# A fused attention and feed-forward kernel: full-array sums, two products in separate banks, differences on GpSimd, a fourth up pair and a split last block

## The chip, the cores and the metric

The kernel runs on one core of one Trainium2 chip. The metric is the device time of one execution in microseconds (us); lower is better. "Span" is the time from the first to the last instruction of the profiled execution, some 1 to 2 us less than the device time of the same run.

## The reference, cut to what matters

Attention with keys and values averaged over groups of 8 tokens, then a feed-forward block whose activation is `h * cos(h)`.

```python
k_p = k.reshape(B, H, Sp, pool, D).mean(axis=3)          # B=8, H=8, S=576, D=64, pool=8: 72 pooled keys
v_p = v.reshape(B, H, Sp, pool, D).mean(axis=3)
attn = softmax(q @ k_p.T / sqrt(D))                      # per batch and head
x = (attn @ v_p).transpose(0, 2, 1, 3).reshape(4608, 512)
h = x @ w_in                                             # 512 -> 2048
out = (h * cos(h)) @ w_out                               # 2048 -> 512
```

## The kernel before

The 4608 tokens go through in nine stages of 512. In a stage the tokens go *up* (64 matmuls of 128x512, 8 groups of 2 banks of PSUM, each group followed by a cosine on ScalarE and a multiply `g_sb` on VectorE) and *down*. From stage 1 on, the down part is a seven-product scheme in place of the eight plain products: sums and differences of quarters of `g_sb` (g1 to g4) times sums and differences of quarters of the weights (w2 to w4). Between the products stands the attention of the next batch, in four units of 4 heads by 256 tokens and a rest of 8 heads by 64: scores, exponential, sums and values, Ln and Exp (which give one over the sum), and the multiply that writes `xT`, the next stage's input. GpSimd loads and pools the keys and values of the batch after.

The buffers of PSUM, and the sums and values. `ones` and `vz` are 64 columns wide here, so two heads sit on the two halves of the output partitions, sums in one bank and values in the other:

```python
    banks = [psum.tile([128, 2, 512], FP32, name=f"bank{i}") for i in range(3)]
    obanks = [psum.tile([128, 512], FP32, name=f"obank{i}") for i in range(2)]
...
    def values_of(parts, later):
        weights = (lambda b, h: ones[:Sp, :]), (lambda b, h: vz[b % 2][:, h // 2, 3 * (h % 2), :])
        for bank in range(2):
            ...
                    nc.tensor.matmul(pair[hp * 64:hp * 64 + 64, bank, ...], lhsT=weights[bank](b, h0 + i), rhs=ex[...])
        ...
            nc.scalar.activation(out=inv, in_=pair[:, 0, 0:w], func=ACTF.Ln)
            nc.scalar.activation(out=inv, in_=inv, func=ACTF.Exp, scale=-1.0)
            later.append(... nc.vector.tensor_mul(out=x_out(b, u, slice(0, 128)), in0=cols(pair[:, 1, :], u), in1=cols(inv, u)))
```

The down part. Four products go to bank A and three to bank B, and the reads between them take partial sums:

```python
        A, Bb = obanks[1], obanks[0]
        products = [(A, True, ...), (A, False, ...), (Bb, True, ...), (A, True, ...), (Bb, False, ...), (A, False, ...), (Bb, False, ...)]
        ...
        reads = [
            lambda: nc.scalar.copy(out=p1, in_=A),
            lambda: nc.scalar.copy(out=o1[:, :, 0:HM], in_=two(A)),
            lambda: add(v16, Bb, p1),
            lambda: add(q15, A, p1),
            lambda: add(o2[:, :, HM:], two(Bb), two(q15)),
            lambda: (add(o1[:, :, HM:], two(A), two(v16)), rows_out(t, 0, o1)),
            lambda: (add(o2[:, :, 0:HM], two(Bb), two(p1)), rows_out(t, 1, o2)),
        ]
```

The softmax here doesn't subtract the row's maximum and nothing guards it: scores larger than these inputs give would overflow.

## Time and profile before

The median was 319.28 us (319.24 to 319.82, 3 runs), the span 318.0 us. The stages, from the first up matmul of one to that of the next:

| part of the span | us |
|---|---|
| start, to the first up matmul | 17.62 |
| stage 0 (no seven products yet) | 35.62 |
| stage 1 (weights combined on VectorE) | 40.00 |
| stages 2 to 6, each | 32.56 |
| stage 7 (little attention left) | 28.06 |
| stage 8, to the end | 33.94 |

A stage is read in two pieces, the up part (13.85 us where nothing holds it) and the rest, called the down part (18.71 us in stages 2 to 6). The page's busy shares and the chain, which the prediction shows, say that TensorE is at work for 91% of the span, and that in a steady stage only three waits of 0.4 to 1.0 us stand in its way. At a change of matmul form the gap is smaller: product 0 starts at 107.08, its 16 matmuls follow at 0.109 us each, up to 108.83, and the scores start at 108.92, 0.09 us later.

### The profile page before, as it was taken

The page shows a single profiled execution, that of the slowest core. Times are in us where ns is not written, and L with a number is a line of the kernel's source. Part 1 is how long each engine was busy: PE and PEld are TensorE (multiplying, and loading weights), DVE is VectorE, ACT ScalarE, POOL GpSimd, SP SyncE. Part 2 cuts the span into 40 slices and gives each one's busy share as a digit, 9 for nine tenths or more (in the row PEclk, how much of TensorE's full clock was granted, in tenths as well). Part 3 has the DMA queues.
Part 4 walks back from the last instruction along what each step waited for, and adds up shares of the span by engine and source line. Part 5 has one row for each costly group of instructions (what it writes and reads, how often), then busy time and mean ns, then how long its engine had stood idle before and what let it go on. Part 6 is the DMA issues. An engine that isn't in the chain of part 4 may idle for free.

```text
span 318.0 us, 5705 instructions
## 1 busy us (share of the span) xinstructions
PE 289.1 (91%) x2320; PEld 180.7 (57%) x2320; DVE 217.7 (68%) x291; ACT 203.7 (64%) x246; POOL 147.4 (46%) x141
## 2 busy tenths in 40 slices
PE   8799999399989997999799989998999899899991
PEld 3445544136764585458645864587457744774580
DVE  5468558999747955695559555995596559647950
ACT  3876993248766777677757776677668766626400
POOL 8362119953992399339943795389600000000000
PEclk9999999869999999999999999999999999999997
DMA  7999995079538872968295919680810050023005
GB/s 157 200 207 207 207 205 127 20 140 141 84 78 150 107 118 66 162 89 136 53 174 70 159 32 188 93 139 14 187 31 0 2 134 2 0 49 85 0 2 132
DMA packets 43850, 32.98 MB, mean 104 GB/s; under 512 B 22064, under 2 KB 38960, under 8 KB 43824
## 3 DMA queue, kind: packets, MB, share of 16 engines
q0 software_dynamic: 19744, 18.07, 36.3%
q1 hardware_dynamic: 24080, 14.56, 22.7%
q8 instruction: 18, 0.29, 0.4%
q14 instruction: 8, 0.07, 0.1%
HBM read 36.70 MB, written 9.44 MB: 145 GB/s over the span
## 4 chain that ended last, share of the span: by engine, by line
PE 73%; DVE 14%; ACT 8%; issue 3%; ACTq 0%; DVEq 0%
PE bank L333 35%; PE obank L409 24%; DVE g_sb L343 5%; PE bank L278 4%; PE obank L346 3%; PE bank L221 2%; ACT cos L340 2%; ACT inv L285 2%; DVE xT L286 2%; ACT inv L284 2%; DVE o_two L417 2%; PE obank L494 1%; DVE w L363 1%; DVE w L362 1%; ACT ex L228 1%
## 5 line engine op out<-in xcount | busy, mean ns | idle before, releaser
L333 PE MATMUL bank<-xT,w_in_sb 128*128 128x512 bf16 x576 | 129.1, 384 | 8.2 <-DVE g_sb L343 4.9
L340 ACT ACTIVATE cos<-bank,half_pi 128x1024 f32<-128x1024 f32 x72 | 79.2, 1113 | 62.9 <-PE bank L333 57.5
L343 DVE TENSOR_TENSOR g_sb<-bank,cos 128x1024 bf16<-128x1024 f32 x72 | 86.6, 1221 | 30.9 <-ACT cos L340 30.9
L333 PEld LDWEIGHTS <-w_in_sb 128*128 128x128 bf16 x576 | 56.5, 98 | 77.4 <-issue 14.2
L150 POOL TENSOR_TENSOR half_sums<-kv_st 72x512 f32<-72x512 bf16 x48 | 59.8, 1271 | 34.1 <-DMA kv_st<-in_k_dram 33.7
L409 PEld LDWEIGHTS <-g 128*128 128x128 bf16 x512 | 49.0, 98 | 7.1 <-issue 1.2
L409 PEld LDWEIGHTS <-g_sb 128*128 128x128 bf16 x384 | 36.7, 97 | 8.8 <-issue 2.3
L228 ACT ACTIVATE ex<-bank 72x1024 bf16<-72x1024 f32 (+1 forms) x40 | 35.6, 928 | 0.8 <-PE bank L221 0.7
L152 POOL TENSOR_TENSOR half_sums<-half_sums 72x512 f32<-72x512 f32 x24 | 33.0, 1396 | 0.0
L284 ACT ACTIVATE inv<-bank 128x512 f32<-128x512 f32 (+1 forms) x31 | 16.7, 538 | 23.9 <-PE bank L278 23.9
L409 PE MATMUL obank<-w_out_sb,g_sb 128*128 128x256 bf16 x256 | 30.7, 272 | 1.0 <-ACT p_sb L419 1.0
L409 PE MATMUL obank<-w,g 128*128 128x256 bf16 x256 | 30.6, 273 | 0.0
L409 PE MATMUL obank<-w_out_sb,g 128*128 128x256 bf16 x256 | 30.6, 273 | 0.0
L286 DVE TENSOR_TENSOR xT<-bank,inv 128x512 bf16<-128x512 f32 (+1 forms) x31 | 19.5, 629 | 11.8 <-ACT inv L285 11.6
L221 PE MATMUL bank<-qT,kk 64*72 64x256 bf16 (+1 forms) x192 | 14.2, 251 | 9.5 <-DVE xT L286 6.2
L314 ACT ACT_TABLE_LOAD x16 | 20.5, 1283 | 1.0 <-PEq L665 0.7
L285 ACT ACTIVATE inv<-inv 128x512 f32<-128x512 f32 (+1 forms) x31 | 18.0, 582 | 1.0
L221 PEld LDWEIGHTS <-kk 64*72 64x72 bf16 x192 | 8.4, 109 | 16.8 <-issue 15.6
L377 DVE TENSOR_TENSOR g<-g,g_sb 128x512 bf16<-128x512 bf16 x32 | 15.5, 484 | 1.1
L155 POOL TENSOR_TENSOR kp<-half_sums 72x512 bf16<-72x512 f32 x12 | 15.7, 1330 | 0.5
L346 PE MATMUL obank<-w_out_sb,g_sb 128*128 128x512 bf16 x64 | 15.7, 380 | 0.0
L417 DVE TENSOR_TENSOR v_sb<-obank,p_sb 128x512 f32<-128x512 f32 x8 | 5.5, 690 | 14.7 <-ACT ex L228 10.7
(80 smaller groups left out, 259.0 us busy)
## 6 DMA issues: line engine op xcount, KB each, us to landing
out_dram<-o_two SPq DMA_DIRECT2D x72, 128.0 KB, 2.4
kv_st<-in_v_dram POOLq DMA_DIRECT2D x8, 576.0 KB, 12.7
kv_st<-in_k_dram POOLq DMA_DIRECT2D x7, 576.0 KB, 7.7
q_b<-in_q_dram POOLq DMA_DIRECT2D x6, 576.0 KB, 9.7
w_in_sb<-in_moe_w_in_dram POOLq DMA_DIRECT2D x4, 512.0 KB, 13.8
w_out_sb<-in_moe_w_out_dram POOLq DMA_DIRECT2D x4, 512.0 KB, 18.2
q_b<-in_q_dram POOLq DMA_DIRECT2D x4, 288.0 KB, 12.5
g_sb<-in_k_dram SPq DMA_DIRECT2D x1, 576.0 KB, 3.5
```

Source lines behind the costliest of these rows:

```text
L150: add(out=s[:, h:h + 2], in0=x[:, h:h + 2, 0:4, :], in1=x[:, h:h + 2, 4:8, :], op=ADD)
L152: add(out=s[:, h:h + 4, 0:2, :], in0=s[:, h:h + 4, 0:2, :], in1=s[:, h:h + 4, 2:4, :], op=ADD)
L221: nc.tensor.matmul(pair[:Sp, bank, c:c + n].rearrange("p (g n) -> p g n", n=64), lhsT=kk[b % 2][half[r], h0 + i, 0:Sp], rhs=att["qT", b][h ...
L228: nc.scalar.activation(out=ex[:, 0:nh * n].rearrange("p (a n) -> p a n", a=2), in_=pair[:Sp, :, 0:nh * n // 2], func=ACTF.Exp, scale=scale ...
L284: nc.scalar.activation(out=inv, in_=pair[:, 0, 0:w], func=ACTF.Ln)
L285: nc.scalar.activation(out=inv, in_=inv, func=ACTF.Exp, scale=-1.0)
L286: later.append(lambda b=b, u=u, pair=pair, inv=inv: nc.vector.tensor_mul(out=x_out(b, u, slice(0, 128)), in0=cols(pair[:, 1, :], u), in1=c ...
L333: nc.tensor.matmul(h[:, j, :], lhsT=w_in_sb[fc // 4][:, ki, (fc % 4) * 128:(fc % 4 + 1) * 128], rhs=xT[:, ki, t * TILE:(t + 1) * TILE], st ...
L340: nc.scalar.activation(out=cos, in_=h, func=ACTF.Sin, bias=half_pi[:, :1])
L343: nc.vector.tensor_mul(out=g_sb[:, 2 * fp:2 * fp + 2, :], in0=h, in1=cos)
L346: nc.tensor.matmul(o, lhsT=g_sb[:, fc, ms * 128:(ms + 1) * 128], rhs=w_out_sb[fc // 4][:, fc % 4, :], start=(fc == 0), stop=(fc == FFCH - 1))
L409: mms.append(lambda bank=bank, first=first, g=g, w=w, fc=fc, p=p: nc.tensor.matmul(bank[:, p * HM:(p + 1) * HM], lhsT=g(fc, p), rhs=w(fc), ...
```

## The change

Its intent: shorten those waits. Sums and values of two heads come from one matmul of 128 columns (`[v | 8]`), two products run in separate banks before any read, the g3 differences leave VectorE, the two output banks serve as a fourth up pair, half the combined weights are made on GpSimd, and the last stage splits its output so that less is left after the last matmul. The core of the diff:

```diff
-    obanks = [psum.tile([128, 512], FP32, name=f"obank{i}") for i in range(2)]
+    opair = psum.tile([128, 2, 512], FP32, name="opair")
+    obanks = [opair[:, i, :] for i in range(2)]
...
     def up_bank(t, fp):
-        return banks[list(up_order(t)).index(fp) % 3]
+        i = list(up_order(t)).index(fp)
+        if t == 0:
+            return banks[i % 3]
+        return (*banks, opair)[i % 4 if i < 7 else 0]
...
-    def put_g3(i):
-        f0, f1 = 4 * i, 4 * i + 4
-        nc.vector.tensor_tensor(out=g3[:, f0:f1], in0=g_part(0, 0, f0, f1), in1=g_part(0, 1, f0, f1), op=SUB)
+    def put_g3(fp):
+        f0, f1 = 2 * fp, 2 * fp + 2
+        nc.gpsimd.tensor_tensor(out=g3[:, f0:f1], in0=g_part(0, 0, f0, f1), in1=g_part(0, 1, f0, f1), op=SUB)
...
-        A, Bb = obanks[1], obanks[0]
+        apart = t == NT - 1
+        if apart:
+            A, Bb = [[banks[i][:, p, 0:HM] for p in range(2)] for i in (1, 2)]
+        else:
+            A, Bb = [[obanks[i][:, p * HM:(p + 1) * HM] for p in range(2)] for i in (1, 0)]
         products = [
             (A, True, part(g_part(0, 0, 0, HF)), of(w_out_sb[0:2])),
-            (A, False, part(g_part(1, 0, 0, HF)), of(w_out_sb[2:4])),
-            (Bb, True, part(g2), of(w2)),
-            (A, True, part(g1), of(w_out_sb[0:2], 1)),
...
+            (Bb, True, part(g_part(1, 0, 0, HF)), of(w_out_sb[2:4])),
+            (A, True, part(g2), of(w2)),
+            (Bb, True, part(g1), of(w_out_sb[0:2], 1)),
...
         reads = [
-            lambda: nc.scalar.copy(out=p1, in_=A),
-            lambda: nc.scalar.copy(out=o1[:, :, 0:HM], in_=two(A)),
...
+            lambda: each(p1, A),
+            lambda: each(o1, Bb, p1, m1, 0),
...
-            if first:
-                values_of(first, later)
-                later.pop(0)()
+            if steady:
+                values(*u2, later)
...
+                if n == 3 and b + 1 < B:
+                    nc.gpsimd.tensor_copy(out=gate, in_=kk[b % 2][0:1, 0, 0:1])
+                    loads(b + 1)
+                if n > 2 and n < 7:
+                    put_g3(n - 3)
```

`values`, which was there before for stage 0, does Ln and the multiply once per half of the partitions. `each` does its copies and adds on VectorE. `gate` is a copy of one element of the pooled keys; it makes GpSimd's queue wait for them before it issues the next loads (in the profile after, 44.7 us of waiting for the transfer of `kk` before its five copies).

More of the change, by code (lines that the diff above doesn't have):

```diff
@@ L267, in values @@
             later.append(mul)
-    def values_of(parts, later):
-        weights = (lambda b, h: ones[:Sp, :]), (lambda b, h: vz[b % 2][:, h // 2, 3 * (h % 2), :])
-        for bank in range(2):
-            for b, u, pair in parts:
-                (c0, n), (h0, nh) = u
-                ex = att["ex", b, u]
-                for i in range(nh):
-                    hp = i % 2
-                    nc.tensor.matmul(pair[hp * 64:hp * 64 + 64, bank, (i // 2) * n:(i // 2 + 1) * n],
-                                     lhsT=weights[bank](b, h0 + i), rhs=ex[:, ex_col(u, i):ex_col(u, i) + n])
-        for b, u, pair in parts:
-            att.pop(("ex", b, u))
-            w = u[1][1] * u[0][1] // 2
-            inv = inverse_tile(w)
-            nc.scalar.activation(out=inv, in_=pair[:, 0, 0:w], func=ACTF.Ln)
-            nc.scalar.activation(out=inv, in_=inv, func=ACTF.Exp, scale=-1.0)
-            later.append(lambda b=b, u=u, pair=pair, inv=inv: nc.vector.tensor_mul(
-                out=x_out(b, u, slice(0, 128)), in0=cols(pair[:, 1, :], u), in1=cols(inv, u)))
     def sums_first(b, u, cs):
@@ L355, in down_out, with put_weights @@
             nc.sync.dma_start(out=rows_of[b_, ORDER[pos]], in_=o[rows])
-    def put_weights():
-        vec = nc.vector.tensor_tensor
-        parts = [[(w[:, :, 0:HM], w[:, :, HM:]) for w in (w_out_sb[i], w_out_sb[i + 2])] for i in range(2)]
-        for i, ((b11, b12), (b21, b22)) in enumerate(parts):
-            yield lambda i=i, x=b22, y=b12: vec(out=w3[i], in0=x, in1=y, op=SUB)
-            yield lambda i=i, y=b11: vec(out=w2[i], in0=w3[i], in1=y, op=ADD)
-            yield lambda i=i, x=b21: vec(out=w4[i], in0=x, in1=w2[i], op=SUB)
+    def put_weights(i, eng):
+        vec = eng.tensor_tensor
+        (b11, b12), (b21, b22) = [(w[:, :, 0:HM], w[:, :, HM:]) for w in (w_out_sb[i], w_out_sb[i + 2])]
+        vec(out=w3[i], in0=b22, in1=b12, op=SUB)
+        vec(out=w2[i], in0=w3[i], in1=b11, op=ADD)
+        vec(out=w4[i], in0=b21, in1=w2[i], op=SUB)
     def put_first_weights(i):
@@ L393, in part @@
             return lambda fc, p: x[:, fc, p * 128:(p + 1) * 128]
-        A, Bb = obanks[1], obanks[0]
+        apart = t == NT - 1
[3 more added lines that the diff above has]
+            A, Bb = [[obanks[i][:, p * HM:(p + 1) * HM] for p in range(2)] for i in (1, 0)]
         products = [
             (A, True, part(g_part(0, 0, 0, HF)), of(w_out_sb[0:2])),
-            (A, False, part(g_part(1, 0, 0, HF)), of(w_out_sb[2:4])),
-            (Bb, True, part(g2), of(w2)),
-            (A, True, part(g1), of(w_out_sb[0:2], 1)),
-            (Bb, False, part(g3), of(w3)),
-            (A, False, part(g4), of(w_out_sb[2:4], 1)),
-            (Bb, False, part(g_part(1, 1, 0, HF)), of(w4)),
+            (Bb, True, part(g_part(1, 0, 0, HF)), of(w_out_sb[2:4])),
+            (A, True, part(g2), of(w2)),
+            (Bb, True, part(g1), of(w_out_sb[0:2], 1)),
+            (A, False, part(g3), of(w3)),
+            (Bb, False, part(g4), of(w_out_sb[2:4], 1)),
+            (A, False, part(g_part(1, 1, 0, HF)), of(w4)),
@@ L404, in down_products @@
         ]
         mms = []
-        for bank, first, g, w in products:
-            for fc in range(HF):
-                for p in range(2):
-                    mms.append(lambda bank=bank, first=first, g=g, w=w, fc=fc, p=p: nc.tensor.matmul(
-                        bank[:, p * HM:(p + 1) * HM], lhsT=g(fc, p), rhs=w(fc),
-                        start=(first and fc == 0 and p == 0), stop=(fc == HF - 1 and p == 1),
-                        skip_group_check=not first))
-        p1, v16, q15 = [msb.tile([128, d_model], FP32, name=n, tag=n, bufs=1) for n in ("p1_sb", "v_sb", "q_sb")]
@@ L415, in down_products @@
-        o1, o2 = [msb.tile([128, 2, d_model], FP32, name="o_two", tag="o_two", bufs=3) for _ in range(2)]
-        two = lambda x: x.rearrange("p (a m) -> p a m", a=2)
-        add = lambda out, in0, in1: nc.vector.tensor_tensor(out=out, in0=in0, in1=in1, op=ADD)
-        reads = [
-            lambda: nc.scalar.copy(out=p1, in_=A),
-            lambda: nc.scalar.copy(out=o1[:, :, 0:HM], in_=two(A)),
-            lambda: add(v16, Bb, p1),
-            lambda: add(q15, A, p1),
-            lambda: add(o2[:, :, HM:], two(Bb), two(q15)),
-            lambda: (add(o1[:, :, HM:], two(A), two(v16)), rows_out(t, 0, o1)),
-            lambda: (add(o2[:, :, 0:HM], two(Bb), two(p1)), rows_out(t, 1, o2)),
+        for n, (bank, first, g, w) in enumerate(products):
+            order = [(fc, p) for fc in range(HF) for p in range(2)]
+            if apart and n == 6:
+                order.sort(key=lambda x: x[1])
+            for fc, p in order:
+                mms.append(lambda bank=bank, first=first, g=g, w=w, fc=fc, p=p: nc.tensor.matmul(
+                    bank[p], lhsT=g(fc, p), rhs=w(fc),
+                    start=(first and fc == 0 and (apart or p == 0)), stop=(fc == HF - 1 and (apart or p == 1)),
+                    skip_group_check=not first))
@@ new lines, in down_products, with each @@
+        p1, v16, q15 = [msb.tile([128, 2, HM], FP32, name=n, tag=n, bufs=1) for n in ("p1_sb", "v_sb", "q_sb")]
+        o1, o2 = [msb.tile([128, 2, d_model], FP32, name="o_two", tag="o_two", bufs=3) for _ in range(2)]
+        m1, m2 = slice(0, HM), slice(HM, d_model)
+        def each(out, bank, other=None, m=slice(0, HM), tk=None):
+            for p in range(2) if apart else (slice(0, 2),):
+                ps = bank[p] if apart else obanks[1 if bank is A else 0].rearrange("p (a m) -> p a m", a=2)
+                if other is None:
+                    nc.vector.tensor_copy(out=out[:, p, m], in_=ps)
+                else:
+                    nc.vector.tensor_tensor(out=out[:, p, m], in0=ps, in1=other[:, p], op=ADD)
+                if apart and tk is not None:
+                    rows_out(t, tk, out, (p,), m, (nc.sync, nc.scalar))
@@ L426, in down_products, with rows_out @@
+        reads = [
+            lambda: each(p1, A),
+            lambda: each(o1, Bb, p1, m1, 0),
+            lambda: each(v16, A, p1),
+            lambda: each(q15, Bb, p1),
+            lambda: each(o2, A, q15, m2, 1),
+            lambda: (each(o1, Bb, v16, m2, 0), apart or rows_out(t, 0, o1)),
+            lambda: (each(o2, A, p1, m1, 1), apart or rows_out(t, 1, o2)),
         ]
         return [mms[i * 2 * HF:(i + 1) * 2 * HF] for i in range(7)], reads
-    def rows_out(t, tk, o):
+    def rows_out(t, tk, o, ps=(0, 1), m=slice(0, d_model), queues=(nc.sync, nc.sync)):
@@ L430, in rows_out @@
         rows_of = out.rearrange("(b p t) m -> b t p m", b=B, t=ROW)
-        for p in range(2):
+        for p in ps:
             for i, rows in enumerate(half):
                 b_, pos = divmod((t * TILE + tk * HT + p * 128) // 64 + i, ROW)
-                nc.sync.dma_start(out=rows_of[b_, ORDER[pos]], in_=o[rows, p])
+                queues[i].dma_start(out=rows_of[b_, ORDER[pos], :, m], in_=o[rows, p, m])
     EX = 4
@@ L525, with loads @@
     sin_tables()
+    def loads(b):
+        load_kv(b, "k", k)
+        load_q(b)
+        load_kv(b, "v", v)
     for t in range(NT):
@@ L547 @@
                 put_first_weights(n // 2 - 1)
-            if 0 < t and n % 2:
-                put_g12(n // 2)
+            if 0 < t:
+                if n % 2:
+                    put_g12(n // 2)
+                if n == 3 and b + 1 < B:
[3 more added lines that the diff above has]
+                    put_g3(n - 3)
             if 0 < t and b < B:
@@ L578 @@
             fi = 0
-            weights = list(put_weights())
             for n, (ms, fc) in enumerate(mms):
@@ L586, with product @@
                     down_out(t, ms, obanks[ms % 2])
-                if n in range(41, 59, 3):
-                    weights.pop(0)()
+                if n == 41:
+                    put_weights(1, nc.vector)
         else:
             products, reads = down_products(t)
-            def product(i):
-                for mm in products[i]:
-                    mm()
+            def product(i, j=0, k=2 * HF):
+                for mm in products[i][j:k]:
+                    mm()
+            if b + 1 < B:
+                pool_add(b + 1, "k")
@@ L596, with scores_of @@
             us = BY_TOKENS
-            steady, rest = b < B, t < B
-            first = [(b, us[i], banks[i]) for i in range(3)] if steady else [(t, REST, banks[1])] if rest else []
-            second = [(b, us[3], banks[0]), (t, REST, banks[1])] if steady else []
-            later = []
-            product(0)
-            reads[0]()
+            later = []
+            u0, u1, u2, u3 = [(b, us[i], banks[j]) for i, j in enumerate((1, 2, 0, 1))]
+            ur = (t, REST, banks[2])
+            def scores_of(*parts):
+                for part in parts:
+                    scores_mm(*part)
+                for part in parts:
+                    scores_exp(*part)
@@ L603, with muls @@
+            def muls():
+                while later:
+                    later.pop(0)()
+            steady, rest = b < B, t < B
             if rest:
                 exp_tables()
-            for part in first:
-                scores_mm(*part)
-            for part in first[:1]:
-                scores_exp(*part)
-            product(1)
+            product(0)
+            product(1, 0, 6)
+            if steady:
+                scores_of(u0, u1, u2)
+            elif rest:
+                scores_of(ur)
@@ L610 @@
+            product(1, 6)
+            reads[0]()
             reads[1]()
-            for part in first[1:]:
-                scores_exp(*part)
-            for i in range(2):
-                put_g3(i)
+            if steady:
+                values(*u0, later)
             product(2)
             reads[2]()
-            put_g4(0)
+            muls()
+            if steady:
+                values(*u1, later)
             product(3)
             reads[3]()
+            muls()
+            put_g4(0)
@@ L620 @@
             put_g4(1)
-            if first:
-                values_of(first, later)
-                later.pop(0)()
+            if steady:
+                values(*u2, later)
             product(4)
             reads[4]()
-            for mul in later:
-                mul()
-            later = []
-            if second:
-                for part in second:
-                    scores_mm(*part)
-                for part in second:
-                    scores_exp(*part)
-            product(5)
@@ L635 @@
-            reads[5]()
-            if second:
-                values_of(second, later)
-                for mul in later:
-                    mul()
+            muls()
+            if steady:
+                scores_of(u3, ur)
+            product(5, 0, 8)
+            if steady:
+                values(*u3, later)
+            elif rest:
+                values(*ur, later)
+            product(5, 8)
+            reads[5]()
+            muls()
+            if steady:
+                values(*ur, later)
@@ L640 @@
+            if b + 1 < B:
+                pool_add(b + 1, "v")
             product(6)
             reads[6]()
+            muls()
         if t < B:
             sin_tables()
-        if 0 < t and b + 1 < B:
-            nc.gpsimd.tensor_copy(out=gate, in_=kk[b % 2][0:1, 0, 0:1])
-        if b + 1 < B:
-            load_kv(b + 1, "k", k)
-            load_q(b + 1)
-            load_kv(b + 1, "v", v)
+        if t == 0:
+            loads(b + 1)
+            put_weights(0, nc.gpsimd)
             pool_add(b + 1, "k")
```

## The prediction

> **What bounds the kernel now.** I read the page first (busy shares, then the chain that ended last), then the chain in order of time, then each engine's timeline over one stage, and last every VectorE instruction with two SBUF inputs against what GpSimd was doing. On the page:
>
> ```profile
> PE 289.1 (91%) x2320; PEld 180.7 (57%) x2320; DVE 217.7 (68%) x291; ACT 203.7 (64%) x246; POOL 147.4 (46%) x141
> PE 73%; DVE 14%; ACT 8%; issue 3%; ACTq 0%; DVEq 0%
> ```
>
> TensorE is the bound on average, but over a quarter of the chain is not TensorE. The chain in time repeats every 32.56 us in the six steady stages (93.23 to 125.80, up to 256.04). One stage:
>
> ```profile
> 93.23 14.02 PE bank L333 x64
> 107.28 1.12 ACT cos L340
> 108.42 1.24 DVE g_sb L343
> 109.70 0.63 PE bank L221 x8
> 110.34 5.40 PE obank L409 x48
> ...
> 119.75 0.61 DVE xT L286
> 120.40 0.33 PE bank L221 x8
> ...
> 124.87 0.42 ACT inv L285
> 125.32 0.44 DVE xT L286
> 125.80 14.02 PE bank L333 x64
> ```
>
> A stage is 13.85 us of up matmuls and 18.72 of down matmuls plus the next batch's attention. TensorE's own work in those 18.72 is some 15.6: seven products of 16 matmuls at 0.109 us (12.25; three follow each other at 110.34, 112.08, 113.83), about 1.0 of scores, 2.1 of sums and values, and small gaps at each change of matmul form. The rest is three waits: 0.38 us for the last `g_sb` multiply before scores (109.70), 1.04 for an `xT` multiply to free a bank (120.40), 0.55 for the last `xT` multiply before the next up (125.80), with their pipeline ends about 3 us a stage. VectorE is busy 21.8 of 32.56 us, ScalarE 23.3.
>
> Two more places. From 51.56 to 61.0 VectorE makes the combined weights, six instructions of 1.27 to 1.75 us, while the up matmuls of stage 1 stand still 4.89 us. And the end: the last matmul is done at 311.18, the last add at 311.89, the span ends at 318.04.
>
> ```profile
> 310.21 4.94 SPq L434 DMA_DIRECT2D out_dram<-o_two  x8
> 311.20 0.69 DVE L417 TENSOR_TENSOR o_two<-obank,p_sb 128x512 f32<-128x512 f32 x1 [1.05 <-PE obank L409]
> ```
>
> The eight last output issues go one after the other from one queue until 315.16, and a landing takes 2.4 us more (page, part 6).
>
> [...]
>
> ```profile
> 63.05 2.48 POOL L152 TENSOR_TENSOR half_sums<-half_sums 72x512 f32<-72x512 f32 x2
> 65.61 1.32 POOL L158 TENSOR_TENSOR vz<-half_sums 72x512 bf16<-72x512 f32 x1
> 64.59 1.23 DVE L376 TENSOR_TENSOR g<-g_sb 128x512 bf16<-128x512 bf16 x1
> 65.85 1.37 DVE L377 TENSOR_TENSOR g<-g,g_sb 128x512 bf16<-128x512 bf16 x1
> ```
>
> Each add, 0.42 us alone, waited for the running GpSimd instruction to end (65.53, 66.93) and finished 0.29 later. Multiplies with one PSUM input kept their 1.22 and 0.69 us beside busy GpSimd. In the stage from 190.92 the adds met GpSimd and VectorE was busy 25.2 instead of 21.8 us, yet the stage still took 32.55: VectorE had slack there. [...]
>
> **The change, part by part.** P is the start of product 0 (107.08 above), 13.85 us after the up start.
>
> *Sums and values over the full array.* 24+24 matmuls with 64 stationary columns, run in pairs, become 24 with 128: 16 at 0.109 and 8 of 64 wide make about 2.0 us against 2.13[...]. The price is on the other engines: sums and values now lie on opposite halves, so Ln and the multiply are done per half. A Ln of 64x512 costs 0.59 as one of 128x512 does, a multiply 0.70 as against 0.69. ScalarE gains 4x0.59+0.37=2.7 us, VectorE 4x0.69+0.43=3.2.
>
> *Two products in separate banks.* Product 1 no longer waits for the copy of product 0. Copy and first add go from ScalarE (0.59+0.57, and a table load of 1.28) to VectorE (2x0.69). Net: ScalarE about +0.3 a stage, nothing.
>
> *Differences on GpSimd.* VectorE loses 2x0.68; GpSimd gains four 128x512 instructions, each an estimate of 1.15 to 1.26 us from its 512-wide adds here. VectorE's net is +3.2+1.4-1.4=+3.2 us, to 25 of 32 us, nearly all in the down part, where it works in order.
>
> *One steady stage by hand, without collisions.* The table is loaded at P+2.6; product 0 and six matmuls of product 1 end at 2.4; scores without a wait (banks 1, 2, 0 free at -0.9, 1.2, 2.6); the three exponentials end at 5.8, Ln and Exp of unit 0 at 7.6. From there VectorE never rests long: four multiplies of 1.31 in spacing, four adds of 0.61, two g4 of 0.64, the last multiply 0.85 make 9.8, and a wait of about 0.2 for unit 3. The next up starts at P+17.65 against 18.72: -1.07. TensorE would have been ready at 15.75.
>
> *The same with GpSimd in the way.* In stages 1 to 5 the differences stand behind the gate and the loads in GpSimd's queue. The gate came 8.9 to 10.6 us after the up start; earlier output issues may make it 8 to 9.7, the three issues take 2.5, so the differences run from 10.4 or 12.2 on, when VectorE does g1 and g2 of the third quarter (13.0), and then the pooling starts (8 us after the gate) and runs to the end of the stage. Third quarter: +0.4 to 1.45. Last quarter: its adds end at about P+5.6 instead of 3.45, the p1 copy at 6.2, product 2 waits for it, and unit 0's multiply starts at 8.8 instead of 7.6. The two g4 take 2.8 instead of 1.3 us (0.57 mean wait, then a whole 1.1, each with 0.55 of own work). Next up at about P+20.0: +1.3 against before.
>
> *Fourth up pair and half the weights on GpSimd.* GpSimd waits 7.78 us for a load before 46.58; three 1024-wide instructions of 2.25 (twice its 512-wide) fit, free. VectorE's weights end at 56.2 instead of 61.0, the multiplies of stage 1 start at 57.4 instead of 62.2, and with four pairs TensorE goes on to its seventh pair unhindered. But the adds then meet the pooling and the differences, so of 4.8 us I keep 1.3 with collisions, 4.6 without.
>
> *Stage 6* has no loads: differences follow their multiplies and slip between the adds, -1.07. *Stage 7*: no wait before scores and none for the p1 copy on ScalarE; 14.2 becomes 13.15, -1.07. *Last blocks apart*: the wait of 0.66 becomes one of 0.8 for the copies in halves, even; but the tail is one 256-wide add (0.42), one issue (0.6) on one of two queues and 2.4 landing, 3.5 against 6.86 us: -3.4.
>
> Sum with collisions: 4x(+1.3) -1.3 -1.07 -1.07 -3.4 = -1.6, 317.6 us. Without: 4x(-1.07) -4.6 -1.07 -1.07 -3.4 = -14.4, 304.9.
>
> **Rivals.** (1) [...] as worked out: 317 to 319. For it: [...] the queue order of the changed kernel puts the differences behind the loads. Against: my gate time is a guess within 2 us; a gate 2 us earlier would let the third quarter through. (2) The collisions mostly miss, or fall into pauses: 305 to 310. For it: before, 3.4 us of them cost nothing. Against: TensorE-side slack is what paid for that, and the change spends it. (3) GpSimd gets late with the pooled keys: its work per stage is 2.5+4.8+9.5+8.2=25 us plus 0.5 per collision, from about 10 us into a stage to 2 us into the next; the keys are due at 6 us into the next, so it should hold; if not, 322 or more. (4) The stage stays TensorE-bound and all waits vanish: 6x3 and the ends, 297; ScalarE's Ln and Exp in a row speak against it.
>
> **Range and chances.** The main account gives 317.6, the other 305. I weigh them about four to one and get 315. The finely split products (6 of 16, 8 of 16) look tuned on a chip, which speaks for a gain that I may underrate. 315.5, range 308 to 321. Under 312.9 is faster by 2%: 0.38; over 325.7: 0.08, through rival 3 alone; within: 0.54.
>
> **What would show it.** Right: in stages 2 to 5 the adds of g1, g2 and g4 take 1 to 1.6 us, VectorE is 25 to 29 us busy, the next up waits for an `xT` multiply at 19 to 20.5 after product 0, stages of 33 to 34.3 us; stage 6 at 31.5; last matmul to end 3.5 us. Wrong: those adds at 0.42 and 0.68, stages under 32, or a wait of `qT` or `kk` before scores.

## The result, and the profile after

The changed kernel is correct and takes 362.64 us (median of 4 runs, 361.29 to 365.23) against 319.26 in the same rounds. The ratio is 1.137 [1.129, 1.144]: it is slower by 14%, and outside the predicted range.

The span grew by 41.4 us to 359.4. Almost every part grew, the ones that the change barely touches included (start and stage 0):

| us | start | stage 0 | 1 | 2 to 5, mean | 6 | 7 | 8 | span |
|---|---|---|---|---|---|---|---|---|
| before | 17.62 | 35.62 | 40.00 | 32.56 | 32.56 | 28.06 | 33.94 | 318.0 |
| after | 19.72 | 42.35 | 42.66 | 38.95 | 35.41 | 32.07 | 31.44 | 359.4 |

Only the last stage is shorter. The page of the changed kernel, busy time of each engine over the span, shows no engine that became a bound by its sum:

```profile
PE 294.6 (82%) x2168; PEld 182.9 (51%) x2168; DVE 247.3 (69%) x326; ACT 205.6 (57%) x254; POOL 189.1 (53%) x176
```

TensorE lost 9 points of its share, and VectorE's share is what it was. So neither is always busy and something makes them wait. The chain that ended last, which carried the reading of before, is no help here: it goes back only to 345.62 us, into the last stage. The waits of TensorE (what waited, on what; us in total, times, longest) give the answer:

```profile
PE opair L398 <- DVE o_two L414: 26.7, 21, 2.7
PE bank L317 <- DVE xT L262: 10.0, 6, 1.7
PE opair L330 <- DVE o_two L335: 5.5, 3, 4.4
PE bank L317 <- DVE g_sb L327: 4.1, 5, 1.5
PE opair L398 <- DVE v_sb L414: 2.8, 7, 0.8
PE opair L398 <- DVE q_sb L414: 2.8, 7, 0.8
```

L398 is the products, L414 the reads of their results. TensorE's products wait 26.7 + 2.8 + 2.8 = 32.3 us for those reads (L330 and L335 are the same pair of roles in stage 0); the kernel before had no such line but 1.0 us on ScalarE's copy. One stage in order of time, first TensorE (start, us, what; in brackets the idle time before and what ended it):

```profile
119.12 2.73 PE L398 MATMUL opair<-w_out_sb,g_sb 128*128 128x256 bf16 x22
...
125.82 1.91 PE L398 MATMUL opair<-w,g 128*128 128x256 bf16 x16 [1.56 <-DVE o_two L414]
127.56 0.60 PE L251 MATMUL bank<-ex,vz 72*128 72x256 bf16 x4
128.51 1.91 PE L398 MATMUL opair<-w_out_sb,g 128*128 128x256 bf16 x16 [0.34 <-DVE v_sb L414]
130.25 0.60 PE L251 MATMUL bank<-ex,vz 72*128 72x256 bf16 x4
131.20 1.91 PE L398 MATMUL opair<-w,g 128*128 128x256 bf16 x16 [0.34 <-DVE q_sb L414]
...
143.61 2.75 PE L317 MATMUL bank<-xT,w_in_sb 128*128 128x512 bf16 x12 [1.67 <-DVE xT L262]
```

and VectorE over the same time:

```profile
121.72 1.43 DVE L359 TENSOR_TENSOR g<-g_sb 128x512 bf16<-128x512 bf16 x1
123.18 1.26 DVE L360 TENSOR_TENSOR g<-g,g_sb 128x512 bf16<-128x512 bf16 x1
124.36 0.68 DVE L412 COPY p_sb<-opair 128x512 f32<-128x512 f32 x1
125.07 0.69 DVE L414 TENSOR_TENSOR o_two<-opair,p_sb 128x512 f32<-128x512 f32 x1
127.76 0.69 DVE L414 TENSOR_TENSOR v_sb<-opair,p_sb 128x512 f32<-128x512 f32 x1 [2.00 <-PE opair L398]
...
130.45 0.69 DVE L414 TENSOR_TENSOR q_sb<-opair,p_sb 128x512 f32<-128x512 f32 x1 [0.57 <-PE opair L398]
```

Follow the clock through both. Product 2 writes the bank that `p_sb` (124.36) read, which was free at 125.04. It starts at 125.82, which is 0.06 us after the end (125.76) of the *other* bank's read, `o_two`. Product 3 writes the bank that `o_two` read, free since 125.76; it starts at 128.51, 0.06 after `v_sb` has read product 2's bank. Product 4 starts 0.06 after `q_sb` has read product 3's. So from product 2 on every product waits for the read of the product just before it. The two banks never work at the same time, and product (1.91) and read (0.69) add up instead of overlapping.

The program that was built says the same. It keeps account of buffers by tile, and two views of one tile share one account. The waits of product 2, for a count of VectorE's instructions, in the programs built from the changed kernel and from e1 below, which has two tiles (these lines are from the built programs, not from the profile; the number is that of the instruction waited for):

```
opair@512  (product 2)   waits for VectorE 285 = o_two <- opair@0,  p1     the other bank's read
obank1@0   (product 2)   waits for VectorE 284 = p1    <- obank1@0         its own bank's read
```

The change does rotate its products through two banks; this trace shows that rotating the addresses is not enough where the waits are kept per tile (product 2 stood 1.56 us, until the other bank's read was done).

The tail, where the kernel before had eight issues in one queue from 310.21 on, now has two queues:

```profile
352.01 4.48 SPq L434 DMA_DIRECT2D out_dram<-o_two  x6
```
```profile
352.02 4.76 ACTq L434 DMA_DIRECT2D out_dram<-o_two  x6
```

The last matmul, by the timeline of TensorE, is done at 354.90, two adds in halves end at 355.69, the issues at 356.78, the span at 359.4: 4.5 us against 6.86 before.

### The profile page after: what moved, and what is told of

Same layout as the page of the kernel before. It is cut to its first block, busy times and chain, and to the rows that moved or that the text cites. A ratio compares the mean times of both kernels' runs of the same rounds, so it can differ in the third digit from the quotient of the medians.

```text
span 359.4 us, 5492 instructions
## 1 busy us (share of the span) xinstructions
PE 294.6 (82%) x2168; PEld 182.9 (51%) x2168; DVE 247.3 (69%) x326; ACT 205.6 (57%) x254; POOL 189.1 (53%) x176
## 3 DMA queue, kind: packets, MB, share of 16 engines
q0 software_dynamic: 19744, 18.07, 32.3%
## 5 line engine op out<-in xcount | busy, mean ns | idle before, releaser
L364 POOL TENSOR_TENSOR g<-g_sb 128x512 bf16<-128x512 bf16 x32 | 38.4, 1208 | 84.1 <-DVE g_sb L327 84.1
L398 PEld LDWEIGHTS <-g 128*128 128x128 bf16 x512 | 51.5, 101 | 40.5 <-issue 32.6
L257 ACT ACTIVATE inv<-bank 64x512 f32<-64x512 f32 (+1 forms) x72 | 39.1, 544 | 41.0 <-PE bank L251 40.1
L262 DVE TENSOR_TENSOR xT<-bank,inv 64x512 bf16<-64x512 f32 (+1 forms) x72 | 45.3, 629 | 6.3 <-ACT inv L258 4.9
L398 PE MATMUL opair<-w_out_sb,g 128*128 128x256 bf16 x224 | 31.6, 295 | 15.9 <-DVE o_two L414 13.1
L398 PEld LDWEIGHTS <-g_sb 128*128 128x128 bf16 x384 | 37.1, 99 | 13.9 <-issue 5.6
L398 PE MATMUL opair<-w,g 128*128 128x256 bf16 x224 | 26.7, 272 | 12.8 <-DVE o_two L414 9.9
L398 PE MATMUL opair<-w_out_sb,g_sb 128*128 128x256 bf16 x224 | 27.6, 273 | 0.6 <-DVE g_sb L327 0.6
L557 POOL COPY gate<-kk 1x1 bf16<-1x1 bf16 x5 | 0.9, 179 | 44.7 <-DMA kk<-kp 44.7
L251 PE MATMUL bank<-ex,vz 72*128 72x256 bf16 (+1 forms) x176 | 21.4, 255 | 0.0
L330 PE MATMUL opair<-w_out_sb,g_sb 128*128 128x512 bf16 x64 | 16.0, 379 | 5.5 <-DVE o_two L335 5.5
L359 DVE TENSOR_TENSOR g<-g_sb 128x512 bf16<-128x512 bf16 x32 | 19.1, 598 | 1.1
L398 PE MATMUL opair<-w,g_sb 128*128 128x256 bf16 x112 | 14.5, 286 | 3.7 <-DVE o_two L414 3.7
```

The source lines that it names most:

```text
L251: nc.tensor.matmul(pair[:, hp, (i // 2) * n:(i // 2 + 1) * n], lhsT=vz[b % 2][:, pj, 2 * hp:2 * hp + 2, :].rearrange("p a d -> p (a d)"), ...
L257: nc.scalar.activation(out=inv[half[1 - hp]], in_=pair[half[1 - hp], hp, 0:w], func=ACTF.Ln)
L262: nc.vector.tensor_mul(out=x_out(b, u, half[hp]), in0=cols(pair[half[hp], hp, :], u), in1=cols(inv[half[1 - hp]], u))
L364: nc.gpsimd.tensor_tensor(out=g3[:, f0:f1], in0=g_part(0, 0, f0, f1), in1=g_part(0, 1, f0, f1), op=SUB)
L398: mms.append(lambda bank=bank, first=first, g=g, w=w, fc=fc, p=p: nc.tensor.matmul(bank[p], lhsT=g(fc, p), rhs=w(fc), start=(first and fc ...
```

## The experiments

Times are medians of 4 runs. The kernel before took 319.39 us (318.63 to 320.83), 319.65, 319.96 and 319.91 in the four sets of rounds. All eleven kernels are correct. The stages of those that the argument uses (spans, one profiled run each):

| us | start | stage 0 | 1 | 2 to 5, mean | 6 | 7 | 8 | span |
|---|---|---|---|---|---|---|---|---|
| e1, two tiles | 17.72 | 35.62 | 42.90 | 36.75 | 34.13 | 28.81 | 31.54 | 337.7 |
| e7, e1 and filler | 17.36 | 36.45 | 42.83 | 35.44 | 32.71 | 27.12 | 31.56 | 329.8 |
| e10, e1, g3 on VectorE | 17.62 | 35.62 | 39.18 | 35.93 | 32.37 | 27.06 | 31.46 | 327.0 |
| e4, e1 and 64-column sums | 16.73 | 36.15 | 42.22 | 33.85 | 32.08 | 27.26 | 31.55 | 321.4 |
| e11, e4, loads after g3 | 17.47 | 35.62 | 37.09 | 34.03 | 33.68 | 27.26 | 31.54 | 318.8 |
| e5, e4, g3 on VectorE | 18.26 | 35.62 | 36.14 | 32.07 | 32.01 | 27.19 | 31.46 | 309.0 |
| e6, e5, multiply first | 17.33 | 36.15 | 35.14 | 31.14 | 30.74 | 27.20 | 31.46 | 302.6 |

My theory after reading the trace was the one tile; the rival was the prediction's own one, collisions of VectorE and GpSimd (an add of 0.42 us alone took 1.23 and 1.37 beside GpSimd's in the kernel before) and the halved Ln and multiply.

### e1: the changed kernel with two tiles again

```diff
-    opair = psum.tile([128, 2, 512], FP32, name="opair")
-    obanks = [opair[:, i, :] for i in range(2)]
+    obanks = [psum.tile([128, 512], FP32, name=f"obank{i}") for i in range(2)]
...
-        return (*banks, opair)[i % 4 if i < 7 else 0]
+        return banks[(i + 2) % 3]
```

> The changed kernel with the two output banks declared as two tiles again, and the up pairs back on three pairs. Theory T1 (one tile makes every product wait for the VectorE read of the OTHER bank): 314 to 322 us, steady stages 33 to 34.3 us as the prediction's collision account had them, no product starting right after the read of the other bank. Rival T2 (the GpSimd/VectorE collisions alone are dearer than I reckoned) and rival T3 (Ln and multiply per half fill ScalarE and VectorE): stays above 350 us, since neither is touched.

Measured: 338.7 us (336.59 to 339.5), ratio to before 1.059 [1.053, 1.064]. The edit takes 23.9 us off, and the start and stage 0 are back at before's lengths (17.72 and 35.62). It changes two things at once, the tile and the fourth up pair; e3 keeps the pair. Of TensorE's waits, those on reads of an output bank are down to the last of these lines, product 2's wait for the copy of its own bank:

```profile
PE bank L316 <- DVE xT L261: 16.5, 6, 2.9
...
PE obank L397 <- DVE p_sb L411: 3.4, 4, 0.8
```

Stage 7, which has almost no attention, shows the cost by itself: its down part takes 32.07 - 13.82 = 18.25 us after and 28.81 - 15.62 = 13.19 in e1, so 5.1 us for five products that wait.

So the one tile is the largest part, but not all: e1 is still 6% slower than before, 17 us above what the theory expected, and the steady stages take 36.75 us and not 33 to 34.3. It waits 16.5 us for the last `xT` multiply before the next up, 2.9 us in a stage.

### e2: the kernel before, with one tile, nothing else changed

```diff
-    obanks = [psum.tile([128, 512], FP32, name=f"obank{i}") for i in range(2)]
+    opair = psum.tile([128, 2, 512], FP32, name="opair")
+    obanks = [opair[:, i, :] for i in range(2)]
```

> The kernel before with only its two output banks put into one tile; nothing else. T1: slower by 2 to 3.5 us in each of six steady stages and by 5 or more in stage 0 and at the end, 340 to 350 us. T2 and T3: 319 us, unchanged.

Measured: 350.67 us (350.37 to 351.24), ratio 1.097 [1.093, 1.101]. The two lines alone cost 31.3 us in the old kernel, 0.7 more than the expected range. By spans the start and stage 0 lose 15.9 of it and stages 2 to 6 lose 2.07 each. Its waits:

```profile
PE opair L347 <- DVE o_two L352: 9.0, 3, 7.8
PE opair L410 <- DVE v_sb L418: 7.4, 8, 1.5
PE opair L410 <- ACT o_two L421: 6.5, 8, 0.9
```

Shown from both sides, then: taking the tile apart helps the new kernel, joining it hurts the old one.

### e3: the fourth up pair without the joint tile

The fourth pair made of two separate tiles, with cosine and multiply of that pair in two halves:

```diff
+        if h is None:
+            for j in range(2):
+                nc.scalar.activation(out=cos[:, j], in_=obanks[j], func=ACTF.Sin, bias=half_pi[:, :1])
+            for j in range(2):
+                nc.vector.tensor_mul(out=g_sb[:, 2 * fp + j, :], in0=obanks[j], in1=cos[:, j])
+            return
```

> The first experiment with the fourth up pair kept, made of the two separate output tiles (cosine and multiply of that pair in two instructions of 512 each). T1: 1 to 3 us faster than with three pairs, mostly in stage 1, where VectorE holds the pairs longest; 313 to 320 us. If the fourth pair itself was the harm, it is slower than the first experiment by over 10 us.

Measured: 335.55 us (334.97 to 336.54), ratio 1.050 [1.046, 1.054]: about 3 us less than e1, as expected of the pair, though with intervals that touch; the time expected, 313 to 320 us, was missed by 15.6. The joint tile was there for this pair: the pair gives 3 us, and with the pair in both kernels the tile takes 27.1 (362.64 to 335.55). The 23.9 of e1 are the difference of the two.

### e4: sums and values with 64 columns again

On e1, each `values` becomes the old form (sums in one bank, values in the other, one Ln and one multiply over 128 partitions), at the new places:

```diff
-                values(*u0, later)
+                values_split(*u0, later)
```

> The first experiment with sums and values as 64-column matmuls again (Ln, Exp and multiply over 128 partitions). T3 in its weaker form (VectorE's order bounds the down part, 3.2 us a stage are from the halves): 1 to 2.5 us a stage faster than the first experiment, 303 to 312 us. If TensorE or the collisions bound it: within 2 us of the first experiment.

Measured: 323.59 us (322.81 to 324.36), ratio 1.013 [1.008, 1.017]. The full-array matmuls with their halved Ln and multiply cost 15.1 us (not tested apart from each other), 2.9 us in each of stages 2 to 5, a little more than the weaker T3 forecast, but from e1's unexpected level, so the time is 11.6 us above the expected range. In e1 VectorE runs without a pause from 157.16 to the next up at 169.79. The end of that row, with multiplies in pairs:

```profile
166.73 1.39 DVE L261 TENSOR_TENSOR xT<-bank,inv 64x512 bf16<-64x512 f32 x2
168.16 0.69 DVE L413 TENSOR_TENSOR o_two<-obank,p_sb 128x512 f32<-128x512 f32 x1
168.88 0.86 DVE L261 TENSOR_TENSOR xT<-bank,inv 64x256 bf16<-64x256 f32 x2
```

The same row in e4, with single multiplies and with pauses in which VectorE waits for TensorE (the next up still waits 1.1 us for the last multiply):

```profile
159.82 0.68 DVE L283 TENSOR_TENSOR xT<-bank,inv 128x512 bf16<-128x512 f32 x1
161.44 0.69 DVE L430 TENSOR_TENSOR o_two<-obank,p_sb 128x512 f32<-128x512 f32 x1 [0.94 <-PE obank L414]
162.04 0.41 DVE L283 TENSOR_TENSOR xT<-bank,inv 128x256 bf16<-128x256 f32 x1
```

This was a cost that the prediction had in its sum; its size is treated below.

### e5: the g3 differences back on VectorE

```diff
-        nc.gpsimd.tensor_tensor(out=g3[:, f0:f1], ...)      # four of 128x512, in the up part
+        nc.vector.tensor_tensor(out=g3[:, f0:f1], ...)      # two of 128x1024, after the second read
```

> The kernel with two tiles and 64-column sums (323.6 us), but with the g3 differences on VectorE in the down part, as before, so that no difference of GpSimd is left; the loads still go out in the middle of the up matmuls. [...] the adds of g1, g2 and g4 take about 0.42 and 0.68 us again wherever GpSimd does not pool, stage 1 comes back to 40 us or under and the steady stages to about 32: 312 to 316 us. Rival: the collisions fall where VectorE has slack, and the two differences put back (2 x 0.68 us a stage) only lengthen its row in the down part: 322 to 330 us.

Measured: 310.32 us (309.86 to 311.02), ratio 0.972 [0.969, 0.974]. It beats the expectation of the first case, that the collisions are what still keeps the kernel behind the one before, by 1.7 us: 13.3 us less than e4, and the first version that beats the kernel before. Stage 1 gains 6.1 us, the steady stages 1.8 each. The mechanism differs a little from the expectation: the differences now meet the pooling themselves and take, in stages 1 to 5, 0.9 to 1.6 us each in place of 0.68. But they do so in the down part, where VectorE has pauses, and the adds of g1 and g2 in the up part are at 0.42 us again with one exception in the steady stages.

### e6: the last multiply before the last add

```diff
-            reads[6]()
             muls()
+            reads[6]()
```

> The kernel of the run before, with one line moved: the last xT multiply goes before the last output add on VectorE. If VectorE's order is what holds the next up matmuls (they waited 1.11 us for that multiply), each of six stages gains about 0.7 to 1.1 us: 4 to 6 us less than the run before, 306 to 311 us. Rival: the multiply itself comes late, from Ln and Exp on ScalarE, and the add in front of it costs nothing: the same time as the run before within 1 us.

Measured: 304.48 us (304.36 to 305.23), ratio 0.954 [0.951, 0.956]. 5.8 us less than e5, 1.5 below the expected range. The waits of the up matmuls for `xT`, 6.7 us in e5, are gone; what is left for them is:

```profile
PE bank L333 <- DVE g_sb L343: 3.9, 6, 1.2
```

This version beats both kernels: 4.6% faster than before, 16% less time than the changed kernel (304.48 against 362.64, medians of different rounds).

### e7: matmuls that nobody reads

In e1's trace the up part, 13.85 us before, took 15.2 to 17.1. The matmuls in it were slow for 3.4 us. By stretches, for the line of the up matmuls (stretch and its length; TensorE's busy time and count; those of its weight loads; granted clock; share of the DMA engines, GB/s):

```profile
132.90:134.20 1.30, 1.28 (x6) 0.60 (x7) 1.00 0.92 203
134.20:137.60 3.40, 3.40 (x9) 1.19 (x8) 0.50 0.98 202
137.60:141.00 3.40, 3.40 (x17) 1.58 (x16) 0.99 0.76 135
```

Nine matmuls in 3.4 us at clock 0.50, and 17 in the same time at 0.99: half of 3.4 us is lost. TensorE had stood still for 2.87 us until 132.92, 1.3 us before this stretch. The test fills the idle time:

```diff
             muls()
+            if steady:
+                for i in range(12):
+                    nc.tensor.matmul(obanks[0], lhsT=w_in_sb[0][:, 0, 0:128], rhs=w_in_sb[0][:, 0, :])
```

> The changed kernel with two tiles (338.7 us), and twelve matmuls of 128x512 after product 6 in each of the six or seven steady stages, into the bank that product 6 does not use; nobody reads them. They only keep TensorE at work while it waits for the last multiply. If the idle of about 3 us before the next up is what halves the granted clock for 3.4 us afterwards, the clock stays at full, each up part takes 13.9 us instead of 15.2 to 17.1, and the kernel takes 328 to 333 us. Rival: the clock falls for another reason[...], so more matmuls do not help: 338 us or more.

Measured: 330.48 us (329.55 to 331.55), ratio 1.034 [1.030, 1.037], 8.2 us less than e1 by doing more work. The up parts took 14.8, 14.8, 15.2, 14.8, 13.9 and 13.9 us in place of 16.1, 16.3, 15.2, 17.1, 15.6 and 15.6; the down parts of stages 2 to 5, 20.55, did not move. What remains above 13.85 is TensorE's wait for late `g_sb` multiplies (6.0 us in all, stage 1 with it). The same place, clock 1.00:

```profile
132.00:135.40 3.40, 3.40 (x16) 1.57 (x17) 1.00 0.90 199
```

The rival, that more matmuls do not help, is out: with more work the mean granted clock of the profiled runs rose from 0.967 to 0.993.

### e8: only the last stage's split, on the kernel before

```diff
-            products, reads = down_products(t)
+            products, reads = (last_products if t == NT - 1 else down_products)(t)
```

`last_products` is the changed kernel's, with the up pairs that are free there.

> The kernel before, with the last stage alone as in the changed kernel: two products in separate banks of the up pairs, output adds in halves, two queues. The prediction took 3.4 us for the tail (6.86 to 3.5 us from the last matmul to the end). If that stands by itself, the last stage goes from 33.94 to about 31 us and the kernel to 315.5 to 317 us, everything before the last stage the same to 0.1 us. Rival: VectorE's halved copies and adds hold up the products by as much as the tail gains: 319 us.

Measured: 317.31 us (316.58 to 318.1), ratio 0.993 [0.990, 0.996]. A gain of 2.3 us, 0.3 short of the expected range. The last stage and the one before it took 59.5 us together in place of 62.0 (one record of an up matmul is missing at their border). In the profiled run the start and stage 1, which the edit does not touch, were also 0.3 and 0.4 us shorter, so "the same to 0.1 us" did not hold. From the last matmul to the end it is 4.5 us, not the 3.5 of the prediction.

### e9: the fourth pair on the best kernel

The edit of e3, on e6.

> The best kernel so far (304.5 us: two tiles, 64-column sums, differences on VectorE, multiply before the last add), with the two output tiles again as a fourth up pair, cosine and multiply in halves there. In the changed kernel with two tiles the fourth pair gave 3.2 us. If it gave that because TensorE could run ahead of a VectorE that collisions had made late, it gives 0 to 1 us here, where the up matmuls run at 13.85 us without a gap: 303.5 to 305. If a fourth pair is worth something by itself, 301 to 303. It costs two smaller instructions in place of one on ScalarE and VectorE, once a stage: at worst 306.

Measured: 304.86 us (304.41 to 305.39), ratio 0.953 [0.950, 0.956]: the same as e6, as the first case expected. In e6, whose up matmuls wait only 3.9 us in all for `g_sb`, the fourth pair is worth nothing.

### e10: halved multiplies without collisions

The edit of e5, on e1.

> The changed kernel with two tiles (338.7 us), keeping Ln and multiply in halves, with the g3 differences on VectorE. With 64-column sums this step took 13.3 us off (323.6 to 310.3). If the two costs add up, 325 to 327 us. If VectorE in its fixed order is the bound with halved multiplies, the two differences of 0.68 us or more put back there eat some of it: 328 to 334 us. If halved multiplies only cost because of collisions, 312 us or under.

Measured: 330.37 us (328.8 to 331.09), ratio 1.033 [1.029, 1.036]. The middle case, 8.3 us. By the spans, stage 1 gives 3.7 us and the up parts, which no longer wait for a late `g_sb` and mostly keep their clock (mean of the span 0.988, in e1 0.967), give 11.2; but the down parts of stages 2 to 5 got longer, from 20.55 to between 20.7 and 22.3 us (4.4 in all), because the two differences now stand in VectorE's full row. So the two costs do not simply add: with halved multiplies VectorE's row is the bound in the down part, and work taken off GpSimd comes back there.

### e11: the differences ahead of the loads

On e4, whose stage 1 held a riddle: an instruction on VectorE (L367, first weights) that takes 0.68 us alone took 3.14. VectorE, then GpSimd, in e4:

```profile
68.24 3.14 DVE L367 TENSOR_TENSOR w_out_sb<-w_out_sb 128x1024 bf16<-128x1024 bf16 x1
```
```profile
68.03 0.78 POOL L94 DMA_DIRECT2D q_b<-in_q_dram  x1
68.80 0.84 POOL L113 DMA_DIRECT2D kv_st<-in_v_dram  x1
69.65 3.85 POOL L380 TENSOR_TENSOR g<-g_sb 128x512 bf16<-128x512 bf16 x3
```

It began 1.4 us before the difference, during the issues of loads, and ended at 71.38, 0.56 after the first of the three differences (70.82). The same instruction took as long at the same place in e1 (3.15 from 68.66) and e7 (3.14 from 69.07). In e5, with the same loads but no difference behind them, it took 0.68 from 68.90, in the middle of the same issues. The edit:

```diff
+                if n > 2 and n < 7:
+                    put_g3(n - 3)
-                if n == 3 and b + 1 < B:
+                if n == 6 and b + 1 < B:
                     nc.gpsimd.tensor_copy(out=gate, in_=kk[b % 2][0:1, 0, 0:1])
                     loads(b + 1)
-                if n > 2 and n < 7:
-                    put_g3(n - 3)
```

> The kernel with two tiles and 64-column sums (323.6 us), with the g3 differences still on GpSimd, but issued ahead of the gate and the three loads instead of behind them. If the prediction's account of the queue was right (the differences run late because they stand behind gate and loads, and so meet the adds of the third and fourth quarter and make a row with the pooling), they now run right after their multiplies: the 3.14 us of the first-weights instruction in stage 1 goes back to about 0.7, stage 1 from 42.2 to 40 us or under, steady stages the same or up to 0.5 us shorter: 317 to 321 us. Rival: the loads and with them the pooling come some 5 us later, and the pooled keys of the next batch are late for the transpose: steady stages of 34 us or more, a wait of the scores for kk, 325 us or more.

Measured: 321.27 us (320.34 to 322.15), ratio 1.006 [1.002, 1.009], 2.3 us less than e4 and 0.3 above the expected range. Stage 1 is 5.1 us shorter (42.22 to 37.09), and no instruction of L367 is over 0.8 us. But an add of g2 there took 2.48 us from 65.85: the pooling that ran when it began ended at 66.94, and it ended only at 68.33, 0.28 us after a difference that had begun at 66.91. So the long hold moved to another instruction. The steady stages did not gain: 34.03 against 33.85, and stage 6 lost 1.6, because the pooling slipped back and its end now meets the adds of the next up part (one taking 1.38 us from 131.50). So where the differences stand in GpSimd's queue decides *which* of VectorE's adds collide, not whether some do. The feared wait for the keys did not come.

## Why the prediction was wrong

**The step that failed.** It is "*Two products in separate banks.* Product 1 no longer waits for the copy of product 0", with the hand account of a steady stage built on it ("From there VectorE never rests long"). The sentence itself holds: in the trace product 1 follows product 0 without a wait (22 matmuls in a row at 119.12). But the account let every later product wait for its own bank alone, so that products and reads overlap and VectorE is never short of work. The diff had made the two banks views of one tile for the sake of the fourth up pair. The built program orders by tile, so product and read of different banks took turns, and VectorE did rest (2.00 and 0.57 us for TensorE at 127.76 and 130.45). I read those two lines of the diff as a change of shape. They cost 27.1 us in the new kernel (e3; 23.9 when the fourth pair goes with them, e1) and 31.3 in the old (e2).

**The rest of the gap, by spans.** The sum with collisions said -1.6 us; the span grew by 41.4. Of the 43.0 between them 21.7 are the edit of e1, the tile less what its fourth pair gave (359.4 - 337.7). The other 21.3 are read from e1, stage by stage against the prediction's own terms:

| term | predicted us | measured in e1 us | missed us |
|---|---|---|---|
| down parts of stages 2 to 5 | 4 x (+1.3) | 4 x (20.55 - 18.71) = 7.4 | 2.2 |
| up parts of stages 2 to 7, clock | 0 | 8.6 | 8.6 |
| up parts of stages 2 to 7, late `g_sb` | 0 | 4.3 | 4.3 |
| stage 1 | -1.3 | +2.9 | 4.2 |
| stage 6, down part | -1.07 | 18.52 - 18.71 = -0.2 | 0.9 |
| stage 7, down part | -1.07 | 13.19 - 14.21 = -1.0 | 0.1 |
| last stage | -3.4 | -2.4 | 1.0 |
| start | 0 | +0.1 | 0.1 |
| sum | -1.6 | +19.7 | 21.3 |

The up parts of e1 are 12.9 us over six times 13.85, those of e7 4.3 over; the difference of 8.6 is put down to the clock (an estimate from the mean granted clocks, 0.967 over the 337.7 us of e1 and 0.993 over the 329.8 of e7, is 8.8).

**What was right.** With two tiles the collided account of a steady stage holds: product 0 at 149.24, unit 0's multiply 8.6 us later (8.8 predicted), the next up 20.55 later (20.0). VectorE in its fixed order is what ends the stage there, as rival 1, the collided account, had it. The adds of g1 and g2 took 1.43 and 1.26 us in collision (the lines at 121.72 and 123.18 above; 1 to 1.6 predicted). The gate came 9.3 us after the up start in e4 (8 to 9.7), and the differences did stand behind the loads. Stage 7's 13.15 was measured as 13.19. The three 1024-wide weights on GpSimd took 2.12 to 2.13 us each in the changed kernel (2.25 was an estimate from the 512-wide adds of before).

**What was mis-sized.** Collisions in the up part were taken as delay of the next product only. They also hold up `g_sb` multiplies and so the up matmuls themselves, 1.1 us in a stage. Stage 1 was thought to keep 1.3 of 4.8 us. Its up part did gain: the multiplies start at 57.94 (57.4 predicted) and it takes 17.18 us in place of 21.28. But its down part takes 25.73 in place of 18.72: product 0 waits 3.9 us for a `g_sb` multiply that stands behind the add of 3.15 us (68.66). With the differences back on VectorE (e10) stage 1 is 3.7 us shorter (42.90 to 39.18). The price of the full-array sums was counted in VectorE's row of the down part only; e4 shows 15.1 us in all for it, by spans 4.2 in the down parts of stages 2 to 5 and 10.8 in the up parts of stages 2 to 7; e4's mean granted clock was 0.988, e1's 0.967. The tail was thought to be 3.5 us from the last matmul to the end: the two adds take 0.79 (0.42 predicted), the issues end 1.09 later (0.6) and the span 2.6 after that (2.4), 4.5 in all. One reading in the prediction is off, without weight for its sum: the chain repeats at 32.56 us in five stages (2 to 6), not six.

**What was missing.** Nothing in the prediction asks what a wait of TensorE does to the matmuls after it. In e1 a wait of 2.87 us was followed, 1.3 us after its end, by 3.4 us at clock 0.50, which cost 1.7 more. The changed kernel itself has five stretches of 3.41 us at clock 0.50 (from 62.16, 96.29, 137.25, 174.80 and 215.76), so a part of what the tile cost is clock too; no run separates it.

**The rivals.** Rival 3 (GpSimd late with the keys) did not come true: in no steady stage of any run did the scores wait for `kk`. Rival 2's 305 to 310 us, and the 304.9 of the sum without collisions, are close to e6's 304.5, but that is luck: e6 got there without the full-array sums, the differences on GpSimd and the fourth pair, on which that sum rests. No version came near rival 4's 297.

**What stays open.** The 3.14 us of e4, repeated in e1 and e7, show a VectorE add held from before a GpSimd instruction's recorded start until after its end. e5 and e10, with the same loads and no difference on GpSimd, have no such hold; e11 has one of 2.48 us with no load in between, so the loads are not needed for it. Why it was held, no view shows. Nor was it shown which waits of TensorE are followed by half clock: in e1 the one of 2.87 us until 132.92 was, while after the one of 2.88 until 169.79 the granted clock was 1.00 (170.00 to 180.00). In stage 1 of the later versions some adds still collide with the pooling; no run took that away. Of the parts of the change that e6 keeps, only the split last stage has a run of its own (e8, 2.3 us); the two products in separate banks, the earlier loads and the weights on GpSimd were not tested one by one.

## What to carry to other kernels

When a change joins two buffers, even only to address them as one, look at which waits the built program gives to each half before believing in any overlap: separate banks with one account acted as one buffer here (27.1 us, e3). Ask of an idle gap of TensorE what it does to the matmuls after it (in e1 one of 2.87 us was followed by a loss of 1.7 more), and prefer a version that has no gap (e7, 8.2 us). Move elementwise work to the other engine only if it doesn't slow the adds that stand on the path (1.43 and 1.26 us in place of 0.42 in the changed kernel; e5, 13.3 us); here the order of two instructions on the busy engine (e6, 5.8 us) was worth more than the fourth pair (3 us at best) or the split last stage (2.3).
